# Thirteen more one-element activations at the head of ScalarE's stream, with written-out engine orders found anew

## The chip, the cores and the metric

The kernel runs on one core of one Trainium2 chip. A core has TensorE (PE; its weight loads are listed as PEld), VectorE (DVE), ScalarE (ACT), GpSimd (POOL) and SyncE (SP), which run their own instruction streams side by side and wait for one another through semaphores; SyncE and ScalarE also issue transfers (DMA) between the chip's main memory and the on-chip memories. The metric is the time of one execution on the device in microseconds (us).

## What is computed

Two 5-tap convolutions over time, each followed by a GELU and by taking every second row, then a joint of a speech transducer. With B = 2, T = 4000, D = 512, K = 5 and U = 8, all in bf16:

```python
h = sum(xp[:, i:i+T] @ w1[i] for i in range(5));  h = gelu(h)[:, ::2]     # T1 = 2000 rows
f = sum(hp[:, i:i+T1] @ w2[i] for i in range(5)); f = gelu(f)[:, ::2]     # T2 = 1000 rows
fe = f @ w_f;  ge = g @ w_g
j = tanh(fe[:, :, None, :] + ge[:, None, :, :])                           # B x 1000 x 8 x 512
out = j @ w_o
```

## The kernel before

**The start.** SyncE loads the first 512 rows of x (`xr`) and the first weights. TensorE runs eight dummy matmuls on constants, then transposes `xr` (`turn`, lines 567 to 587) into PSUM, the accumulator memory. VectorE and ScalarE copy the transposes to `eo`: VectorE the first part, ScalarE three copies. The first two of those, with VectorE's, are what the first real matmuls read (`direct`, line 766, tap 0); the third is read later, with taps 1 and 3. ScalarE runs one activation of a single element ahead of that (`warm`, line 499: it writes `warm[0:1]` from `warm[1:2]`, a scratch), which also loads the table of the GELU.

**The convolutions.** Most of both convolutions is computed by a fast algorithm on sums and differences of rows and of tap weights. `w1part` (line 631) and `w2part` (line 611) make the weights: `tt` steps on VectorE, and doublings (`scaled`, line 606) that either ScalarE or VectorE may run. `Triple.step` (line 669) makes the sums of rows (tiles `row`, `xp`, `xa`), again with doublings of either engine. A `Unit` (line 699) is one block of 128 output channels: five groups of matmuls into two PSUM banks, evicted between them by ScalarE (tile `sd`, then the GELU into `hT`) and VectorE (`acc`, `sd`).

**The joint.** ScalarE makes the tanh tiles `jT` and `jX`. The product with `w_o` is done on blocks of 4 x 128 rows by a seven-product scheme (`Seven`, line 1069): sums of tanh blocks (`sums`, tile `ss`) on GpSimd or VectorE, sums of `w_o` (`tw`), seven products on TensorE, results kept in `sn` or written to the output tile `og` by ScalarE or VectorE, and stores of `og` issued by SyncE. Single blocks of 128 rows in between go straight (`Plain`, tile `ost`). At the end (lines 1268 to 1273) the last `Seven` splits its last store between ScalarE's queue and SyncE's, and the last 128 columns of the last plain block are evicted and stored by ScalarE.

**What sets the order.** The program first records every step with what it reads and writes (`Plan`), and works out from that which step waits for which: a step waits for the semaphore of any step, of its own engine too, whose result it reads or whose tile it overwrites (`edges`, line 155). The order in which each engine runs its steps is not that of the recording: it is written out in full in `ORDER` (line 16), one list for each engine, as differences of step numbers. A step that may run on either of two engines (`flex`) runs on the one in whose list it stands. So an engine's list says both what it runs and in which order, and a step that has to wait holds up all behind it on its engine.

Of the kernel before, what the change touches and what calls it, by code (L numbers as in the profile page):

```python
# [7 lines left out]
ACT = mybir.ActivationFunctionType  # L8
# [6 lines left out]

ORDER = {
    "pe": """
# [13 lines left out]
        1 6 3 3 1 4 2 3""",  # L31
    "act": """
# [8 lines left out]
        91 -68 101 -95 96 -83 -8 25 -3 32 -23 25 -36 16 8 3 14 6 5 9 3 10 6 21 -8 14 10 3 10 6 10 3 8 6 6 3 12 7 1 8 1""",  # L41
    "dve": """
# [9 lines left out]
        -13 19 18 74 -52 -13 20 16 -9 6 -27 43 7 6 2 19 -7 13 15 -3 9 8 2""",  # L52
    "pool": """
        1 42 1 -42 1 1 1 15 218 1 -217 258 -252 253 8 89 174 150 1 54 -2 1 -31 33 33 2 -1 38 -36 35 40 -38 37 34 2 33
        -32 33 32 -30 31 1 1 33 1 28 1 1 28 155 -154 1 27 2 -1 33 -31 32 1 28 2 -1 31 -29 30 1 26 37 -36 37 1 1 33 34
        -33 34 -32 33 1 29 2 -1 33 2 -1 33 -31 32 1 34 2 35 2 27 -26 27 1 1 24 1 28 -26 29""",
    "sp": """
        6 2 1 1 1 1 1 1 1 1 1 1 1 2 2 1 1 1 1 2 1 1 1 1 1 248 1 1 1 1 1 1 2 1 1 1 1 1 254 1 1 145 3 33 33 4 1 1 30 4 33
        4 1 1 33 4 31 4 1 1 29 4 29 4 1 1 29 4 25 4 1 1 25 4 25 4 1 1 27 4 27 4 1 1 25 4 25 4 1 1 19 1 11 4 21 11 4 19
        11 4 17 11 1 1 4 17 11 1 1 4 17 11 4 1 1 19 11 4 21 1 11 4 25 4 23 1 1 4 23 4 19 1 1 7 3 3 5 5""",  # L60
}
# [254 lines left out]
def bass_standalone__seq2seq_rnn_t_joint__speech_kernel(  # L316
# [35 lines left out]
    BU = B * U  # L352
    NT = 512
    NWARM = 8
    TAPS = (0, 4, 2, 1, 3)
    NX = 2

    with ExitStack() as es:
        cur = [16512]

        def at(name, shape, dtype, offset=None):
            o = cur[0] if offset is None else offset
            b = Buf(nc, name, shape, dtype, o)
            if offset is None:
                cur[0] = (b.end + 31) // 32 * 32
            return b
# [29 lines left out]
        warm = at("warm", [2], FP32)  # L396
# [52 lines left out]
        def act(o, i, func, scale=1.0, bias=None):  # L449
            rd = (i,) if bias is None else (i, bias)  # L450
            pl.op("act", lambda e: e.activation(o.ap, i.ap, func, scale=scale,  # L451
                                                bias=0.0 if bias is None else bias.ap), rd, (o,),
                  o.ap.free_size() * 0.833e-3 + (0.05 if i.psum else 0.105 if bias is None else 0.186))
# [22 lines left out]
        def load_w(eng, dst, src, slack=0.0):  # L476
            return pl.dma(eng, lambda e: e.dma_start(dst.ap, src), (), (dst,), slack=slack)
# [4 lines left out]
        def load_xr(rt, after=None):  # L482
            n = NR[rt]
            dst = xr[rt][0:n].map(lambda a: a.rearrange("p r k c -> p (r k c)"))
            src = x[0, 4 * P * rt:4 * P * rt + n * P, :].rearrange("(p r) c -> p (r c)", r=n)
            o = pl.dma("sp", lambda e: e.dma_start(dst.ap, src), (), (dst,), nbytes=n * P * 1024, rate=370e3)  # L486
            if after is not None:
                o.after.append(after.idx)
            return o
# [6 lines left out]
            return pl.dma("sp", lambda e: e.dma_start_transpose(out=dst.ap, in_=src), (), (dst,), nbytes=n * 2 * D, rate=175e3, slack=slack)  # L496

        came = [load_xr(0)]
        act(warm[0:1], warm[1:2], ACT.Gelu_apprx_tanh)

        def load_w1(i, after=None):
            o = load_w("sp", w1_sb[i], w1[i].rearrange("(k c) d -> c k d", c=P), 0.5 if i == TAPS[1] else 0.2)
            if after is not None:
                o.after.append(after.idx)
            return o
# [3 lines left out]
        def load_a(*phs, after=None):  # L509
            for ph in phs:  # L510
                o = load_x6(xa, 0, ph, JA, 0, 16 * -(-(NF + 2) // 16), 0.8)
                if after is not None:
                    o.after.append(after.idx)

        came.append(load_w1(TAPS[0]))
        came.append(load_w1(TAPS[1]))
        came.append(load_xr(1, came[0]))
        came.append(load_w1(TAPS[2], came[0]))
        load_a(4, 0, after=came[1])
        came.append(load_w1(TAPS[3], came[-3]))  # L520
        load_a(2)
        came.append(load_w1(TAPS[4], came[-3]))
        load_a(1, 3, 5)
# [22 lines left out]
        def warm_mm(n):  # L546
            one = nc.const_aps.tensor(1.0, [P, NT], BF16)
            zz = View(one, np.zeros(0, np.int64), False)
            z = zz.map(lambda a: a[:, 0:P])
            for i in range(n):  # L550
                mm(ps.cols(0, NT), [(z, zz)], True, True)
                pl.ops[-1].cost = 0.43

        warm_mm(NWARM)
        psb = ps.h[:, :].bitcast(BF16)
# [748 lines left out]
```

## Time and profile before

| what | us |
|---|---|
| median of 3 runs (251.9 to 252.15) | 252.02 |
| the profiled execution | 251.77 |
| its span, first to last instruction | 249.9 |
| TensorE busy | 243.4 |
| VectorE busy | 207.8 |
| ScalarE busy | 196.8 |
| GpSimd busy | 100.6 |

The profile is of one execution. Its times count from the start of the span; the rest of the execution's own time, 1.9 us, lies outside the span. Busy time leaves out instructions that only wait or that issue transfers; the rows of issues have a q behind the engine (SPq, ACTq). A timeline row has the start, the length, the engine, the line of the kernel, the operation, and tiles written and read; in brackets stands the time that the engine idled before it and what it waited for. A row with x3 merges three instructions. The granted clock of TensorE was full throughout (0.999).

### The profile page before, as it was taken

How to read it: one execution, taken by the hardware profiler on the slowest of the kernel's cores; microseconds unless marked ns; L12 is line 12 of the kernel's file. 1: busy time of each engine (PE TensorE's matmuls, PEld its weight loads, DVE VectorE, ACT ScalarE, POOL GpSimd, SP SyncE). 2: the span in 40 equal slices, each digit the busy share in tenths (PEclk: the TensorE clock that was granted, in tenths of full speed). 3: DMA queues.
4: the chain of work that ended last, by engine and by line, in shares of the span. 5: the costliest groups of instructions: out<-in, count | busy, mean ns of one | idle time of the engine just before them, and what ended most of it. 6: DMA issues, size and time to landing. Idle time of an engine off the chain costs nothing.

```text
span 249.9 us, 5265 instructions
## 1 busy us (share of the span) xinstructions
PE 243.4 (97%) x1938; PEld 182.9 (73%) x1944; DVE 207.8 (83%) x369; ACT 196.8 (79%) x338; POOL 100.6 (40%) x107
## 2 busy tenths in 40 slices
PE   7999999999999999999999999999999999999992
PEld 3979976666666666666557887777888877878872
DVE  1799996967999993996857989769999999996962
ACT  4787868458795575533799999999999999997661
POOL 1000000000000000000008998969899999998510
PEclk9999999999999999999999999999999999999999
DMA  7999999999000070000001142232453656455465
GB/s 243 295 216 180 175 182 172 188 161 357 8 3 0 0 244 12 0 3 0 1 3 42 64 150 84 88 111 99 147 171 122 198 160 211 132 192 163 146 204 165
DMA packets 54871, 31.83 MB, mean 127 GB/s; under 512 B 31902, under 2 KB 54590, under 8 KB 54846
## 3 DMA queue, kind: packets, MB, share of 16 engines
q1 hardware_dynamic: 54558, 31.34, 47.7%
q8 instruction: 15, 0.25, 0.5%
q10 hardware_dynamic: 288, 0.16, 0.2%
q14 instruction: 10, 0.08, 0.1%
HBM read 7.60 MB, written 16.38 MB: 96 GB/s over the span
## 4 chain that ended last, share of the span: by engine, by line
PE 88%; ACT 5%; DMA 2%; DVE 1%; issue 1%; ACTq 1%; SPq 0%; DVEq 0%
PE acc L459 88%; ACT jT L451 2%; DMA w_sb<-in_w_dram 2%; ACT og L560 1%; ACT sn L560 1%; ACT jX L451 1%; ACTq L1037 1%; DVE og L446 1%; DVE sn L561 0%; DVE og L561 0%; PE acc L596 0%; SPq L486 0%; ACT ost L451 0%; DVEq L277 0%; ACTq L277 0%
## 5 line engine op out<-in xcount | busy, mean ns | idle before, releaser
L446 DVE TENSOR_TENSOR og<-acc,sn 128x512 bf16<-128x512 f32 x84 | 54.9, 680 | 6.6 <-PE acc L459 6.4
L451 ACT ACTIVATE jT<-feT,geT 128x1000 bf16<-128x1000 f32 (+5 forms) x60 | 57.4, 1015 | 0.3 <-DVE feT L446 0.3
L1091 POOL TENSOR_TENSOR ss<-jT 128x512 f16<-128x512 bf16 x34 | 39.4, 1176 | 35.2 <-DVE ss L1091 33.4
L459 PE MATMUL acc<-tw,ss 128*128 128x256 f16 x336 | 46.4, 273 | 0.0
L459 PE MATMUL acc<-row,w_sb 128*128 128x334 bf16 (+2 forms) x224 | 39.0, 297 | 0.0
L459 PEld LDWEIGHTS acc<-tw,ss 128*128 128x128 f16 x336 | 32.4, 98 | 7.5 <-ACT sn L560 0.5
L459 PE MATMUL acc<-wo_sb,jT 128*128 128x256 bf16 (+1 forms) x205 | 33.3, 283 | 0.2
L560 ACT ACTIVATE sn<-acc 128x512 f32<-128x512 f32 x49 | 30.3, 626 | 3.0 <-PE acc L459 2.8
L451 ACT ACTIVATE hT<-acc 128x334 bf16<-128x334 f32 (+3 forms) x36 | 15.4, 432 | 16.6 <-PE acc L459 16.0
L459 PEld LDWEIGHTS acc<-row,w_sb 128*128 128x128 bf16 x224 | 21.3, 97 | 9.2 <-DVE acc L602 0.7
L561 DVE COPY sn<-acc 128x512 f32<-128x512 f32 x35 | 23.8, 683 | 4.5 <-PE acc L459 4.2
L451 ACT ACTIVATE sd<-acc 128x334 f32<-128x334 f32 (+2 forms) x48 | 20.6, 432 | 6.3 <-PE acc L459 4.9
L459 PEld LDWEIGHTS acc<-wo_sb,jT 128*128 128x128 bf16 x208 | 20.3, 98 | 5.0
L443 POOL MEMSET hT<- 128x8 bf16 (+2 forms) x6 | 0.8, 148 | 55.2 <-ACT hT L451 42.9
L1091 POOL TENSOR_TENSOR ss<-ss,jT 128x512 f16<-128x512 f16 x18 | 21.0, 1172 | 2.7 <-DVE ss L1091 2.3
L1091 POOL TENSOR_TENSOR ss<-jT,ss 128x512 f16<-128x512 bf16 x17 | 20.0, 1177 | 2.1 <-DVE ss L1091 2.1
L446 DVE TENSOR_TENSOR row<-row 128x1336 bf16<-128x1336 bf16 (+2 forms) x24 | 18.9, 803 | 0.0
L602 DVE SCALAR_TENSOR_TENSOR acc<-acc,sd 128x334 f32<-128x334 f32 (+2 forms) x24 | 11.7, 486 | 8.1 <-PE acc L459 8.0
L451 ACT ACTIVATE jX<-feT,geT 128x1000 bf16<-128x1000 f32 (+3 forms) x20 | 18.2, 956 | 0.0
L459 PE MATMUL acc<-xp,w_t 128*128 128x334 bf16 (+1 forms) x96 | 17.6, 305 | 0.0
L459 PE MATMUL acc<-hT,w_t 128*128 128x334 bf16 x96 | 17.6, 304 | 0.0
L459 PE MATMUL acc<-wo_sb,ss 128*128 128x256 bf16 x112 | 17.3, 273 | 0.0
(130 smaller groups left out, 469.7 us busy)
## 6 DMA issues: line engine op xcount, KB each, us to landing
out_dram<-og SPq DMA_DIRECT2D x42, 256.0 KB, 2.2
w_sb<-in_w_dram SPq DMA_DIRECT2D x10, 512.0 KB, 5.9
out_dram<-og SPq DMA_DIRECT2D x14, 128.0 KB, 2.0
out_dram<-ost SPq DMA_DIRECT2D x10, 128.0 KB, 2.0
xr<-in_x_dram SPq DMA_DIRECT2D x1, 512.0 KB, 3.6
wf_sb<-in_w_f_dram SPq DMA_DIRECT2D x1, 512.0 KB, 4.1
wg_sb<-in_w_g_dram SPq DMA_DIRECT2D x1, 512.0 KB, 5.2
wo_sb<-in_w_o_dram SPq DMA_DIRECT2D x1, 512.0 KB, 7.6
```

The lines of the kernel that those rows point to most:

```text
L443: pl.op("pool", lambda e: e.memset(v.ap, 0.0), (), (v,))
L446: pl.op(eng, lambda e: e.tensor_tensor(out=o.ap, in0=a.ap, in1=b.ap, op=op), (a, b), (o,), 0.02 + 2.14e-3 * o.ap.free_size() if eng == "po ...
L451: pl.op("act", lambda e: e.activation(o.ap, i.ap, func, scale=scale, bias=0.0 if bias is None else bias.ap), rd, (o,), o.ap.free_size() * ...
L459: ins = e.matmul(o.ap, lhsT=l.ap, rhs=r.ap, start=start and n == 0, stop=stop and n == len(pairs) - 1, skip_group_check=not check)
L560: pl.flex({"act": (lambda e: e.activation(o.ap, v.ap, ACT.Copy), 0.05 + n * 0.833e-3), "dve": (lambda e: e.tensor_copy(out=o.ap, in_=v.ap) ...
L561: "dve": (lambda e: e.tensor_copy(out=o.ap, in_=v.ap), 0.065 + n * 1.04e-3)}, (v,), (o,))
L602: pl.op(eng, lambda e: e.scalar_tensor_tensor(out=o.ap, in0=a.ap, scalar=f, in1=b.ap, op0=ALU.mult, op1=add), (a, b), (o,), vec_cost(o, (a ...
L1037: pl.dma(eng, lambda e, s=s, dst=dst: e.dma_start(dst, s.ap), (s,), (), sem_of(key), 2 * n * P * 4)
L1091: fn = lambda e, o=S[i], x=x, y=y, op=op: e.tensor_tensor(out=o.ap, in0=x.ap, in1=y.ap, op=op)
```

## The change

`NPRE = 14` one-element activations stand where one stood. All later steps of the recording have numbers 13 higher, and the five written-out orders are new.

```diff
@@ bass_standalone__seq2seq_rnn_t_joint__speech_kernel
     NWARM = 8
+    NPRE = 14
     TAPS = (0, 4, 2, 1, 3)
...
         came = [load_xr(0)]
-        act(warm[0:1], warm[1:2], ACT.Gelu_apprx_tanh)
+        for _ in range(NPRE):
+            act(warm[0:1], warm[1:2], ACT.Gelu_apprx_tanh)
@@ ORDER, the head of ScalarE's list and the tail of GpSimd's
     "act": """
-        7 41 2 7 37 6 3 3 -41 50 9 9 -16 2 -5 12 2 -5 12 -3 9 -51 1 1 1 65 11 15 -23 16 -40 25 41 -39 31 -15 9 -23 26 6
...
+        7 1 1 1 1 1 1 1 1 1 1 1 1 1 41 2 7 37 6 3 3 -41 50 9 9 -16 2 -5 12 2 4 9 -6 -45 1 1 1 65 11 15 -23 16 -15 41 -8
...
-        -33 34 -32 33 1 29 2 -1 33 2 -1 33 -31 32 1 34 2 35 2 27 -26 27 1 1 24 1 28 -26 29""",
+        -33 34 -32 33 1 29 2 -1 33 2 -1 33 2 -1 35 2 -1 36 2 -1 28 -26 27 1 27 1 27 1 1""",
```

With the shift of 13 taken out, the lists of before and after compare so (steps by their numbers of before):

| engine | steps before, after | what differs |
|---|---|---|
| TensorE | 696, 696 | the order of eight steps in the first 37 us and of a dozen in the last 32 us |
| ScalarE | 339, 350 | 13 new activations; the order of a dozen steps from 15 to 37 us and of some twenty-five from 206 us on; hands over doublings 123 and 240 and evictions 1412, 1448, 1470, 1573; takes evictions 1397, 1400, 1434, 1533 |
| VectorE | 369, 371 | the order of some forty steps from 11 to 36 us and of some thirty from 215 us on; takes the six steps that ScalarE hands over and hands over the four that it takes; takes sums 1394, 1530, 1554, 1555, 1583 from GpSimd |
| GpSimd | 103, 103 | the order of the last seventeen; takes sums 1462, 1499, 1556, 1584, 1585 from VectorE |
| SyncE | 138, 138 | nothing |

Step 123 is the doubling of a block of tap 1 (`w1part`, line 649); step 240 is the doubling of one row block for the third `Triple` (`step`, line 673). Among VectorE's moved steps, the sums of taps 1 and 3 (`w1part`, lines 647 and 648) change places with row sums (`step`, line 687): three of them now come directly behind the row step that began at 15.76 us. Late in the program, VectorE's output additions of step numbers 1540, 1553 and 1569 (tile `og`) stand behind steps that they preceded.

More of the change, by code (lines that the diff above doesn't have):

```diff
@@ L28 @@
         1 2 1 2 1 2 1 2 7 1 2 1 3 1 7 1 2 1 2 1 2 1 2 7 1 2 1 3 1 5 1 2 1 2 1 2 1 2 7 1 2 1 5 1 5 1 2 1 2 1 2 1 2 7 1 2
[2 rows of a table removed]
-        1 6 3 3 1 4 2 3""",
[2 rows of a table added]
+        4 2 3""",
     "act": """
[8 rows of a table removed]
-        91 -68 101 -95 96 -83 -8 25 -3 32 -23 25 -36 16 8 3 14 6 5 9 3 10 6 21 -8 14 10 3 10 6 10 3 8 6 6 3 12 7 1 8 1""",
-    "dve": """
[9 rows of a table removed]
-        -13 19 18 74 -52 -13 20 16 -9 6 -27 43 7 6 2 19 -7 13 15 -3 9 8 2""",
[9 rows of a table added]
+        3 12 7 1 8 1""",
+    "dve": """
[9 rows of a table added]
+        7 6 17 67 -61 18 -37 46 35 -29 4 17 36 -10 3 -36 13 16 27 7 -21 27 15 -3 9 8 2""",
     "pool": """
-        1 42 1 -42 1 1 1 15 218 1 -217 258 -252 253 8 89 174 150 1 54 -2 1 -31 33 33 2 -1 38 -36 35 40 -38 37 34 2 33
+        1 55 1 -55 1 1 1 28 218 1 -217 258 -252 253 8 89 174 150 1 54 -2 1 -31 33 33 2 -1 38 -36 35 40 -38 37 34 2 33
         -32 33 32 -30 31 1 1 33 1 28 1 1 28 155 -154 1 27 2 -1 33 -31 32 1 28 2 -1 31 -29 30 1 26 37 -36 37 1 1 33 34
-        -33 34 -32 33 1 29 2 -1 33 2 -1 33 -31 32 1 34 2 35 2 27 -26 27 1 1 24 1 28 -26 29""",
+        -33 34 -32 33 1 29 2 -1 33 2 -1 33 2 -1 35 2 -1 36 2 -1 28 -26 27 1 27 1 27 1 1""",
     "sp": """
-        6 2 1 1 1 1 1 1 1 1 1 1 1 2 2 1 1 1 1 2 1 1 1 1 1 248 1 1 1 1 1 1 2 1 1 1 1 1 254 1 1 145 3 33 33 4 1 1 30 4 33
+        6 15 1 1 1 1 1 1 1 1 1 1 1 2 2 1 1 1 1 2 1 1 1 1 1 248 1 1 1 1 1 1 2 1 1 1 1 1 254 1 1 145 3 33 33 4 1 1 30 4 33
         4 1 1 33 4 31 4 1 1 29 4 29 4 1 1 29 4 25 4 1 1 25 4 25 4 1 1 27 4 27 4 1 1 25 4 25 4 1 1 19 1 11 4 21 11 4 19
```

47 rows, old and new, of the table ORDER are left out of this document.

## Prediction

> **What bounds the kernel now.** I read the page first, for the engines' shares and the chain that ended last.
>
> ```profile
> span 249.9 us, 5265 instructions
> PE 243.4 (97%) x1938; PEld 182.9 (73%) x1944; DVE 207.8 (83%) x369; ACT 196.8 (79%) x338; POOL 100.6 (40%) x107
> PE 88%; ACT 5%; DMA 2%; DVE 1%; issue 1%; ACTq 1%; SPq 0%; DVEq 0%
> ```
>
> TensorE is busy for 97% of the span, and 88% of the chain is its matmuls. Their number and shapes do not change. So time can be won or lost in three places only: before the first real matmul, in holes between matmuls, and after the last one. Busy time by stretch (time, then PE, PEld, DVE, ACT, POOL with their counts) shows how much room the other engines leave.
>
> ```profile
> 20.00:30.00 10.00, 10.00 (x115) 10.00 (x113) 9.81 (x23) 8.64 (x20) 0.24 (x2) 1.00 1.14 181
> 240.00:250.00 10.00, 5.33 (x45) 4.03 (x43) 3.99 (x8) 2.90 (x6) 0.00 (x0) 0.98 0.53 171
> ```
>
> From 20 to 30 us TensorE and VectorE are both full. At the end nothing is full: TensorE works 5.33 us of the last ten. The chain of work, in order of time, says what the end waits for, and the timeline of the last microseconds gives the neighbours.
>
> ```profile
> 244.95 2.44 ACTq L1037
> ...
> 247.50 0.28 ACT ost L451
> ```
>
> ```profile
> 244.12 1.26 PE L459 MATMUL acc<-wo_sb,jX 128*128 128x256 bf16 x12
> 244.94 0.38 SPq L1037 DMA_DIRECT2D out_dram<-og  x1
> 245.65 0.33 SPq L1037 DMA_DIRECT2D out_dram<-ost  x1
> 247.80 0.34 ACTq L1037 DMA_DIRECT2D out_dram<-ost  x1
> ```
>
> TensorE ends at 245.38 (244.12 + 1.26). ScalarE's last eviction (ost, 128x128) could start then, but stands behind a store that ScalarE itself issues, and that issue lasts 2.44 us, against 0.38, 0.33 and 0.34 us for the three others here. It releases ScalarE at 247.39, so the last store is issued at 247.80 and the program ends 2.15 us later. About 2.06 us (2.44 less 0.38) of the end is this one long issue.
>
> **Why that issue is long, as far as the trace tells.** The DMA view of just this stretch (244.95 to 247.39 us):
>
> ```profile
> GB/s 369 353 336 370 286 353 403 336 265 353 290 319 315 256 248 407 336 302 386 302 261 143 42 0 29 197 319 420 369 302 336 185 51 17 34 17 34 0 0 0
> q14 instruction: 1, 0.01, 0.8%
> out_dram<-og SPq DMA_DIRECT2D x1, 128.0 KB, 2.4
> ```
>
> Then the instruction queues of the whole program; two issues of SyncE, each followed by the instruction queue that moves something beside it (143.45 to 143.75 and 177.0 to 177.5 us); and the busy times of one stretch around another transfer:
>
> ```profile
> q8 instruction: 15, 0.25, 0.5%
> q14 instruction: 10, 0.08, 0.1%
> 143.49 2.21 SPq L1037 DMA_DIRECT2D out_dram<-og  x1
> q8 instruction: 1, 0.02, 37.2%
> 176.45 1.28 SPq L1037 DMA_DIRECT2D out_dram<-og  x1
> q14 instruction: 1, 0.01, 6.2%
> 187.00:187.40 0.40, 0.40 (x6) 0.29 (x3) 0.40 (x2) 0.40 (x2) 0.18 (x1) 1.00 0.78 271
> ```
>
> Instructions arrive by DMA: 15 transfers on one queue and 10 of 8 KB on the other. Exactly one of the ten falls inside the long issue. SyncE's two longest issues of stores, 2.21 and 1.28 us, also lie beside instruction transfers. The other eight transfers of q14 fall beside compute: in the 0.40 us around each, as around 187.0 us here, ScalarE and VectorE are busy for 0.38 to 0.40 us. They stall nothing. My reading is that a DMA issue is held while the block that follows it is being fetched, and an ordinary instruction is covered by the one that is executing. In the built program ScalarE's stream grows from 462 to 477 instructions of 64 bytes, and the long issue moves from the 454th to the 469th place. An 8 KB block is 128 instructions, so the boundary now comes some 15 instructions ahead of that issue, around 236 us, among evictions.
>
> [...]
>
> **The change part by part.** *The fourteen activations.* Thirteen are new. All write the same element, so each waits for the one before. Rows: the tiny activation of before, the next ScalarE work, a pair on VectorE of which the second waits for the first, and TensorE's weight load for the first real matmul.
>
> ```profile
> 2.03 0.20 ACT L451 ACTIVATE warm<-warm 128x1 f32<-128x1 f32 x1
> 4.89 0.66 ACT L451 ACTIVATE eo<-acc 128x256 bf16<-128x256 bf16 x2 [2.66 <-PE acc L575]
> 7.29 1.67 ACT L608 ACTIVATE hw<-w_sb 128x512 bf16<-128x512 bf16 x3 [0.81 <-DMA w_sb<-in_w_dram]
> 39.44 0.52 DVE L602 SCALAR_TENSOR_TENSOR acc<-acc,sd 128x336 f32<-128x336 f32 x1 [2.48 <-PE acc L459]
> 39.99 0.51 DVE L446 TENSOR_TENSOR sd<-acc,sd 128x336 f32<-128x336 f32 x1
> 6.02 0.35 PEld L459 LDWEIGHTS acc<-eo,w_sb 128*128 128x128 bf16 x4 [0.78 <-ACT eo L451]
> ```
>
> The wait between dependent steps is 0.03 us (39.99 less 39.96). So a tiny step takes 0.23 to 0.24 us, and thirteen take 3.0 to 3.1. The cover is the 2.66 us that ScalarE waits for TensorE's transposes. The last tiny step ends at 2.23 + 3.1 = 5.3, and the first copy starts at 5.2 to 5.35 in place of 4.89. The first two copies, which end at 5.55 (4.89 + 0.66), gate the first real matmul; they now end at 5.9 to 6.0. TensorE's weight load comes at 6.02, and needs a weight that lands shortly before. So the step costs 0 to 0.05 us; I take 0. The third copy is made good in the 0.81 us that ScalarE waits ahead of 7.29. If the dependent step were free, nothing changes; if it costs 0.28 us, the first matmul is 0.5 us late, and everything behind it.
>
> *The first 40 us in the new order.* On SyncE nothing changes place; GpSimd changes only late. Eight steps of TensorE, some forty of VectorE and a dozen of ScalarE do. Two doublings go from ScalarE to VectorE: a w_t (line 649) around 15 us and a row (line 673) around 36 us. The second falls into VectorE's idle 2.48 us ahead of 39.44 and costs nothing. The first lands in a full stretch. On VectorE, the step that needs the last tap's weights (w_t, line 648) moves up to stand right behind the row step of 15.76, and seven steps come ahead of the first unit's evictions.
>
> ```profile
> 7.63 0.29 DVE L609 TENSOR_SCALAR hw<-w_sb 128x512 bf16<-128x512 bf16 x1
> 10.41 0.58 SPq L477 DMA_DIRECT2D w_sb<-in_w_dram  x1
> w_sb<-in_w_dram SPq DMA_DIRECT2D x1, 512.0 KB, 6.3
> 15.76 0.59 DVE L446 TENSOR_TENSOR row<-row,xa 128x832 bf16<-128x832 bf16 x1
> 16.77 0.42 DVE L446 TENSOR_TENSOR w_x<-w_sb 128x512 bf16<-128x512 bf16 x1
> 27.91 0.38 DVE L602 SCALAR_TENSOR_TENSOR acc<-acc,sd 128x206 f32<-128x206 f32 x1 [0.18 <-PE acc L459]
> 30.03 0.85 DVE L446 TENSOR_TENSOR xp<-xp 128x1344 bf16<-128x1344 bf16 x1
> 30.94 0.46 PE L459 MATMUL acc<-xp,w_x 128*128 128x336 bf16 x2
> ```
>
> The doubling adds up to 0.29 us on VectorE. The last tap's weights land at 10.41 + 6.3 = 16.71. Before, their first use was at 16.77. Now it is next at about 16.5 (15.76 + 0.59 and most of 0.29), so VectorE waits some 0.2 us. Of these 0.5 us the idle 0.18 us at 27.91 absorbs a part, and the rest, 0.2 to 0.3 us, reaches the xp step of 30.03. That step ends at 30.88, and the matmul that reads it starts at 30.94: no slack. The other gates, by the same sums (the sd additions, the w_x of the third unit, the row differences), come up to 0.1 us late but ahead of 30.94 and are part of the same delay. So TensorE loses 0.2 us (bounds 0 and 0.35), and, being full, does not make it good.
>
> *The last 35 us in the new order.* Four evictions go from VectorE to ScalarE and four the other way, five sums go from GpSimd to VectorE and five back.
>
> ```profile
> 200.00:220.00 20.00, 19.89 (x160) 15.73 (x162) 19.54 (x33) 20.00 (x27) 20.00 (x18) 1.00 0.52 169
> L560 ACT ACTIVATE sn<-acc 128x512 f32<-128x512 f32 x24 | 14.9, 621 | 3.0 <-PE acc L459 2.8
> L561 DVE COPY sn<-acc 128x512 f32<-128x512 f32 x11 | 7.5, 681 | 0.7 <-PE acc L459 0.6
> ```
>
> An eviction costs 0.62 us on ScalarE and 0.68 on VectorE, so the exchange is even. TensorE has only 0.11 us of holes from 200 to 220 us, which bounds what better orders can win. Laid out by these durations, each eviction still ends before the matmul that needs its bank, the tightest by under 0.1 us. I take 0.1 us of loss (bounds: 0.1 gained, 0.6 lost).
>
> *The end.* With the issue at 0.38 us, ScalarE is free at 245.33, evicts at 245.42, and issues its last store at 245.75. Then SyncE's 128 KB store of 245.65 is last. The last store of before, 32 KB, took 2.15 us from issue to the end; 96 KB more, at the 330 GB/s of the stretch, take 0.3 us, and ScalarE's two stores, which now share that time, up to 0.5. The end is 245.65 + 2.15 + 0.3 = 248.1 to 248.6; I take 248.4, so 1.5 us are won (bounds 0 and 1.8).
>
> *Sum.* 0 + 0.2 + 0.1 - 1.5 = -1.2 us. The profiled execution took 251.77 us, 1.87 more than its span, so its like would take 250.6. The median of the runs is 252.02, 0.25 above it, by which I would say 250.8. I predict 250.7 us.
>
> **The rivals.** *The long issue stays.* It is the first store that ScalarE issues, and may be slow for that reason; no other first issue on that queue is in the trace. For it: the boundary of a block need not stall anything, since the eight transfers beside compute stalled nothing. Against it: SyncE's first issue takes no more than its others, and its two longest lie beside instruction transfers. Then only the 0.3 us are left: 252.02 + 0.3 = 252.3.
>
> *Tiny steps beyond the cover, and the long issue stays* (the slower side). The place is the first copy, and the point from which it decides is 0.24 us for a dependent tiny step: each 0.01 above it delays the first matmul by 0.13. At 0.28 us it is 0.5 us, and the time 252.02 + 0.3 + 0.5 = 252.8. For it: the cover is used up to within 0.1 us. Against it: the 0.03 us between dependent steps.
>
> *The gain is half eaten at the end.* In the new order VectorE makes three output additions of the groups before the last 3 to 5 us later, and SyncE issues its stores in a fixed order, so some 1.5 MB leave between 238 and 243 us, which at 330 GB/s is 4.5 us of full queues; or an eviction misses its matmul. At 0.8 us of cost the time is 251.5.
>
> **How the numbers follow.** The forecast, 250.7, gets 0.58; the issue that stays, 252.3, gets 0.24; both that and the late start, 252.8, get 0.08; the half-eaten gain, 251.5, gets 0.10. A measurement of this kernel can tell some 0.2% from no change, so faster is below 251.5 and slower above 252.5. The forecast and half of the last case are faster: 0.63. Three quarters of the issue that stays are within 0.2%, and with the other half of the last case that makes 0.23. The late start and the last quarter of the issue that stays are slower: 0.14. The range runs from the best bounds of the terms, 250.0 (1.8 won, 0 lost, from the profiled execution), to 252.4, where the second case is mostly in.
>
> **What would show it.** Right: an issue of ScalarE's store of about 0.4 us around 245.2, the last ScalarE eviction right behind TensorE's end, a chain that ends with a SyncE store, and one instruction transfer near 236 us among evictions. The start is right if the first real matmul is at 6.05 to 6.1 and the first 336-column matmul at 31.1 to 31.2. Wrong: an issue still of 2.4 us with no instruction transfer in it (a slow first issue), a first real matmul after 6.3, or holes on TensorE after 216 us of over 0.3 us.

## The result, and the profile after

The changed kernel takes **250.52 us** (median of 4 runs, 250.43 to 250.88) against 252.09 us for the kernel before in the same comparison (4 runs, 251.9 to 252.21). The ratio is 0.9944, with a 95% interval of 0.9932 to 0.9955. That is 1.57 us less in the medians. The profiled executions differ by 1.22 us (251.77 and 250.55), and it is these that can be taken apart. First the page of the changed kernel: the span, the busy times and the shares of the chain that ended last.

```profile
span 248.7 us, 5271 instructions
PE 243.8 (98%) x1938; PEld 182.6 (73%) x1944; DVE 208.0 (84%) x371; ACT 197.6 (79%) x349; POOL 100.7 (41%) x107
PE 86%; ACT 7%; DMA 2%; issue 1%; DVE 1%; SPq 0%; DVEq 0%; ACTq 0%
```

The share of ACTq (ScalarE's DMA issues) in the chain is 0%, where the kernel before had 1%. The last steps of the chain of work and the timeline of the last microseconds show why (start, duration, engine, line, what).

```profile
242.61 3.01 PE acc L461 x23
...
245.65 0.28 ACT ost L453
```

```profile
244.34 1.26 PE L461 MATMUL acc<-wo_sb,jX 128*128 128x256 bf16 x12
...
245.16 0.39 SPq L1040 DMA_DIRECT2D out_dram<-og  x1
245.17 0.38 ACTq L1040 DMA_DIRECT2D out_dram<-og  x1
245.65 0.28 ACT L453 ACTIVATE ost<-acc 128x128 bf16<-128x128 f32 x1 [0.51 <-PE acc L461]
245.87 0.33 SPq L1040 DMA_DIRECT2D out_dram<-ost  x1
245.96 0.35 ACTq L1040 DMA_DIRECT2D out_dram<-ost  x1
```

The issue that took 2.44 us takes 0.38. The last eviction now waits for TensorE (0.51 us, released by its last matmul) and not for ScalarE's own store. TensorE's last group starts at 244.34 in place of 244.12, so everything ahead of the end has become 0.22 us longer. From TensorE's end to the end of the span it is 3.13 us (245.60 to 248.73), where it was 4.57 (245.38 to 249.95): 1.44 us won. 1.44 - 0.22 is the 1.22 us of the profiled executions.

Where the instruction transfer went is seen in two short stretches of the DMA view: 238.2 to 238.8 us, and the issue itself, 245.17 to 245.55 us.

```profile
q14 instruction: 1, 0.01, 4.5%
```

```profile
q1 hardware_dynamic: 149, 0.14, 104.9%
```

In the issue there is only the stores' own queue. The 8 KB transfer that lay in it is at 238.41 us, among evictions, and nothing stalls there: from its start to its end at 238.85 us, TensorE, VectorE and ScalarE are each busy for the whole 0.44 us. The two traces also tell which of the ten 8 KB transfers are ScalarE's. Six begin within 0.5 us of where they began before. Four have moved with its stream, from 40.76, 122.73, 187.10 and 245.87 us to 30.35, 111.84, 182.17 and 238.41 us; in both traces the last of them begins when 448 of ScalarE's rows (waits and issues counted) have started. The long issue was the 448th row, and the short one is the 463rd. (The built program counts six instructions more ahead of each: 454 and 469.)

The start, on ScalarE, and TensorE's first real matmuls:

```profile
2.03 3.25 ACT L453 ACTIVATE warm<-warm 128x1 f32<-128x1 f32 x14
5.18 1.55 ACT L453 ACTIVATE eo<-acc 128x256 bf16<-128x256 bf16 x3
7.83 1.67 ACT L611 ACTIVATE hw<-w_sb 128x512 bf16<-128x512 bf16 x3 [1.10 <-DMA w_sb<-in_w_dram]
```

```profile
5.88 1.38 PE L461 MATMUL acc<-eo,w_sb 128*128 128x254 bf16 x11 [0.69 <-ACT eo L453]
```

Fourteen dependent steps fill 3.25 us. The first copy follows without a gap, 0.29 us later than before, and it now releases the first matmul, at 5.88 us. Before, the first weights released it, at 6.05:

```profile
6.05 1.15 PE L459 MATMUL acc<-eo,w_sb 128*128 128x254 bf16 x9 [0.64 <-DMA w_sb<-in_w_dram]
```

### The profile page after: what moved, and what is told of

The parts are those of the page before. It is cut to its first block, busy times and chain, and to the rows that moved or that the text cites. A ratio compares the mean times of both kernels' runs of the same rounds, so it can differ in the third digit from the quotient of the medians.

```text
span 248.7 us, 5271 instructions
## 1 busy us (share of the span) xinstructions
PE 243.8 (98%) x1938; PEld 182.6 (73%) x1944; DVE 208.0 (84%) x371; ACT 197.6 (79%) x349; POOL 100.7 (41%) x107
## 4 chain that ended last, share of the span: by engine, by line
PE 86%; ACT 7%; DMA 2%; issue 1%; DVE 1%; SPq 0%; DVEq 0%; ACTq 0%
PE acc L461 86%; ACT jT L453 3%; DMA w_sb<-in_w_dram 2%; ACT sn L563 1%; ACT og L563 1%; ACT jX L453 1%; DVE og L448 1%; ACT sd L453 1%; DVE sn L564 0%; DVE og L564 0%; PE acc L599 0%; ACT fT L453 0%; SPq L479 0%; SPq L488 0%; ACT ost L453 0%
## 5 line engine op out<-in xcount | busy, mean ns | idle before, releaser
L563 ACT ACTIVATE sn<-acc 128x512 f32<-128x512 f32 x48 | 29.7, 628 | 3.4 <-PE acc L461 2.8
L564 DVE COPY sn<-acc 128x512 f32<-128x512 f32 x36 | 24.6, 685 | 6.3 <-PE acc L461 6.0
L1094 POOL TENSOR_TENSOR ss<-ss,jT 128x512 f16<-128x512 f16 x19 | 22.3, 1179 | 2.4 <-DVE ss L1094 1.9
L1094 POOL TENSOR_TENSOR ss<-jT,ss 128x512 f16<-128x512 bf16 x15 | 17.5, 1169 | 2.4 <-DVE ss L1094 2.4
```

The costliest lines, as they stand in the source:

```text
L563: pl.flex({"act": (lambda e: e.activation(o.ap, v.ap, ACT.Copy), 0.05 + n * 0.833e-3), "dve": (lambda e: e.tensor_copy(out=o.ap, in_=v.ap) ...
L564: "dve": (lambda e: e.tensor_copy(out=o.ap, in_=v.ap), 0.065 + n * 1.04e-3)}, (v,), (o,))
L1094: fn = lambda e, o=S[i], x=x, y=y, op=op: e.tensor_tensor(out=o.ap, in0=x.ap, in1=y.ap, op=op)
```

## Theories and experiments

**Theory P (place).** The issue was long because it stood at the place of ScalarE's stream where the next 8 KB block of instructions is fetched. The tiny activations are worth something only as a shift. **Rival O (order):** the new order changed what runs and leaves beside the issue. **Rival F (first):** the first store of ScalarE's queue is slow by itself; the changed kernel's own trace, with a first store of 0.38 us, already speaks against it. For the 0.22 us lost ahead of the end, **E** (the early orders) stands against **L** (the landing of the first loads, which differs by execution); **T, C, D** and **S** are refinements that came up on the way.

### 1. The shift alone

```diff
-    act(warm[0:1], warm[1:2], ACT.Gelu_apprx_tanh)
+    for _ in range(14):
+        act(warm[0:1], warm[1:2], ACT.Gelu_apprx_tanh)
     # ORDER as before, indices behind 7 shifted by 13
```

> The kernel before with its own order of steps on every engine, and only the thirteen additional tiny activations behind the first one. ScalarE's first store moves from the 454th to the 467th place of its stream. Theory P (place: the issue is long because it stands where ScalarE's next 8 KB block of instructions is fetched): the issue takes about 0.38 us, the program ends about 3.1 us behind TensorE's last matmul as in the changed kernel (before: 4.57 us), the time is 252.09 - 1.47 = 250.6 us, and down to 250.3 us if the new orders' 0.22 us come off the changed kernel's 250.52. Theory O (order: the issue became short because the new order changed what runs and leaves beside it): the issue stays at 2.4 us and the time is 252.1 to 252.2 us. Theory F (the first store of ScalarE's queue is slow by itself) also gives 2.4 us. For the start: the first real matmul comes within 0.1 us of the kernel before if the thirteen steps (0.234 us each) are covered.

Measured: 250.81 us (6 runs, 250.16 to 251.78) against 252.37 (12 runs), ratio 0.9932 (0.9905 to 0.9959). The end, in the timeline:

```profile
246.16 0.38 ACTq L1044 DMA_DIRECT2D out_dram<-og  x1
246.64 0.28 ACT L457 ACTIVATE ost<-acc 128x128 bf16<-128x128 f32 x1 [0.51 <-PE acc L465]
```

The old orders with the shift have the short issue, and the span ends 3.13 us behind TensorE (246.59 to 249.72), as in the changed kernel. Theories O and F fall. The first real matmul starts at 5.88 us, 0.17 ahead of the kernel before, so the thirteen steps cost nothing there. This execution is late by another cause: TensorE is 1.2 us behind the kernel before by the first matmul of 336 columns. One piece of that is a wait for weights:

```profile
17.56 0.33 PE L465 MATMUL acc<-eo,w_sb 128*128 128x378 bf16 x1 [0.17 <-DMA w_sb<-in_w_dram]
```

Another wait for a load follows on VectorE:

```profile
28.34 0.87 DVE L452 TENSOR_TENSOR row<-row,xp 128x1352 bf16<-128x1352 bf16 x1 [0.63 <-DMA xp<-in_x_dram]
```

The orders are those of before, so these waits are no effect of an order. They are the first sign of theory L.

### 2. The orders alone

```diff
-    NPRE = 14
+    NPRE = 1
     # ORDER of the changed kernel, indices behind 7 shifted back by 13
```

> The changed kernel with one tiny activation in place of fourteen; its orders of steps are kept. ScalarE's first store stands at the 456th place, two behind that of the kernel before. Theory O: the issue takes 0.38 us and the time is that of the changed kernel, 250.5 us. Theory P: the place where the block is fetched now lies on the eviction two instructions ahead, about 0.6 us earlier. If the fetch holds whatever issue stands behind it until it is complete (2.44 us from reaching the place), the issue takes about 1.8 us and the time is 252.1 + 0.2 - 0.6 = 251.7 us; if only the instruction at the place itself is held, the issue takes 0.38 us and the time is 250.5 us.

Measured: 251.2 us (7 runs, 250.72 to 251.52), ratio 0.9946 (0.9923 to 0.9969).

```profile
245.12 1.72 ACTq L1043 DMA_DIRECT2D out_dram<-og  x1
246.95 0.28 ACT L456 ACTIVATE ost<-acc 128x128 bf16<-128x128 f32 x1 [1.85 <-DMA out_dram<-ost]
```

The issue is still long, 1.72 us, close to the 1.8 us of theory P with a hold that goes on until the fetch is complete. (The bracket of the eviction names a store; ScalarE itself was held by its issue until 246.85.) The two places that this order happens to shift the stream are worth the 0.72 us by which the issue is shorter. The time, 251.2 us, lies between the two forecasts, 250.5 and 251.7, and the medians differ by 1.17 us from the kernel before; where the rest of that comes from is not shown.

### 3. One place

```diff
-    act(warm[0:1], warm[1:2], ACT.Gelu_apprx_tanh)
+    for _ in range(2):
+        act(warm[0:1], warm[1:2], ACT.Gelu_apprx_tanh)
```

> The kernel before with one additional tiny activation: everything on ScalarE one place later, orders unchanged. Theory P: the fetch falls on the short wait just ahead of the issue. If the fetch holds what stands behind it, the issue still takes 1.8 to 2.4 us and the time is 251.9 to 252.1 us; if only the very place is held, 0.38 us and 250.6 us. Theory O and theory F: 2.4 us, 252.1 us.

Measured: 251.08 us in one run.

```profile
245.16 1.56 ACTq L1043 DMA_DIRECT2D out_dram<-og  x1
```

One place changes the issue by 0.88 us, with the orders untouched. It was expected between 1.8 and 2.4 us if held and is 1.56: the transfer came at 245.03, ahead of the issue. The time is below the 251.9 to 252.1 us of that case too; it is one run.

### 4. A whole block

```diff
-    act(warm[0:1], warm[1:2], ACT.Gelu_apprx_tanh)
+    for _ in range(129):
+        act(warm[0:1], warm[1:2], ACT.Gelu_apprx_tanh)
```

> The kernel before with 128 additional tiny activations, orders unchanged: ScalarE's first store stands 128 places later, one whole 8 KB block. Theory P: it is again at the place of a fetch and takes about 2.4 us. A theory by which any shift of the stream, or more instructions ahead of it, make the issue short, gives 0.38 us. For the start: the first copy begins at 2.03 + 129 x 0.234 = 32.2 us in place of 4.89, so the whole is some 27.3 us longer, 279.4 us with the long issue and 277.9 us without it, less what the late start saves in waits for loads (up to 1 us).

Measured: 279.89 us in one run (279.4 expected).

```profile
2.03 30.21 ACT L459 ACTIVATE warm<-warm 128x1 f32<-128x1 f32 x129
32.15 1.55 ACT L459 ACTIVATE eo<-acc 128x256 bf16<-128x256 bf16 x3
...
273.11 2.42 ACTq L1046 DMA_DIRECT2D out_dram<-og  x1
```

At 128 places the long issue is back, 2.42 us, with a transfer of 8 KB at 274.01 in it. A shift as such does not cure it: the place counts, and 128 instructions on it comes again. The trace has eleven transfers of 8 KB in place of ten, one more for 128 instructions more (64 bytes each, by this quotient), and the last begins when 576 of ScalarE's rows have started, 128 more than in the kernel before. The time itself is no close comparison: TensorE's mean granted clock was 0.951 in this run, against 0.999 in the kernel before. The same rows price the tiny step: 129 of them in 30.21 us, 0.234 us each from start to start.

### 5 to 8. The parts of the orders, on one chip

Four kernels share the runs of the kernel before (252.22 us, 26 runs).

```diff
 5: the changed kernel again
 6: NPRE = 14  ->  NPRE = 8, ORDER of the changed kernel
 7: NPRE = 8, early part of ORDER from before, last part from the changed kernel
 8: NPRE = 8, ORDER of before throughout
```

> The changed kernel once more, as the yardstick of the three beside it on the same chip. Two views of its first 30 us compete. Theory E (early orders): in the changed kernel TensorE ran 0.08 us behind the kernel before at its 144th matmul and 0.30 us behind at its 300th, and this is the price of the new early orders. Theory L (landings): it is the landing of the first loads, which differs from one execution to the next; with the orders of before but more tiny activations TensorE was 0.15 to 1.2 us behind too (0.21 with one more, 1.21 with thirteen more). For this run both expect 250.5 us and an issue of 0.38 us; theory E a delay between the 144th and the 300th matmul of 0.2 us again, theory L one that differs.

> The changed kernel with eight tiny activations in place of fourteen. ScalarE's first store stands at the 463rd place, nine behind that of the kernel before, and the place of the fetch lies on an eviction about 3 us ahead of it. By the theory of the place, the hold (2.44 us from reaching the place) is over by then and the issue takes 0.38 us; a theory by which it takes all fourteen gives up to 2.4 us. The tiny activations end 1.4 us earlier (six times 0.234), so the first copy waits for TensorE again. If fourteen are covered the time is that of the changed kernel beside it, within 0.05 us; if the first copy was late, it is up to 0.1 us less.

> As the run with eight tiny activations, but every engine has the order of the kernel before up to the middle of the program and the new order in the last 35 us. Issue 0.38 us by the theory of the place. Theory E: 0.2 to 0.3 us less than the run with eight tiny activations and both new orders. Theory L: no difference that exceeds the spread of the runs.

> The kernel before with seven additional tiny activations and its own orders throughout. ScalarE's first store stands at the 461st place, seven behind. Issue 0.38 us by the theory of the place. The late orders alone tell it from the run with the late orders: there TensorE won 0.08 us in the last 35 us of the changed kernel's profile, so this one is expected 0.1 us slower than that, with the bounds of the prediction 0.6 us faster and 0.1 us slower. Theory O gives 252.1 us.

| run | us (median, range, runs) | ratio to before (95%) | issue us | hole at 22.9 to 23.2 us | delay, 144th to 288th matmul (counted from 0) |
|---|---|---|---|---|---|
| 5: changed, 14 tiny | 250.70 (250.01 to 252.05, 9) | 0.9929 (0.9897 to 0.9961) | 0.38 | 0.18 | 0.30 |
| 6: changed, 8 tiny | 250.82 (250.06 to 253.36, 12) | 0.9936 (0.9909 to 0.9963) | 0.40 | 0.22 | 0.34 |
| 7: early orders of before, 8 tiny | 250.40 (250.05 to 253.02, 12) | 0.9941 (0.9909 to 0.9973) | 0.38 | none | 0.28 |
| 8: all orders of before, 8 tiny | 250.46 (250.05 to 250.81, 6) | 0.9920 (0.9889 to 0.9950) | 0.38 | none | 0.08 |

The issue is short in all four, at four distances from the place (15, 9, 10 and 7 instructions). The times do not tell the orders apart: the lowest runs are 250.01 to 250.06 in all four, and the ranges overlap. The traces do, in part. The hole (time from one matmul's start to the next above its usual 0.09 us) is in every execution with the new early orders, and in none with the old. The delay over a longer stretch does not separate them: 0.28 us in run 7 and 0.63 in run 1 with old early orders, 0.08 in run 8. So both theories hold a part: E some 0.1 to 0.25 us, L from 0 to more than the whole effect. The traces show L as VectorE's wait for rows of x: 0.63 us in run 1 (at 28.34) and 0.21 us in run 7 (at 27.93), and none in runs 3, 5, 6 and 8.

The start with eight tiny activations (run 6):

```profile
2.03 1.84 ACT L456 ACTIVATE warm<-warm 128x1 f32<-128x1 f32 x8
5.02 1.70 ACT L456 ACTIVATE eo<-acc 128x256 bf16<-128x256 bf16 x3 [1.15 <-PE acc L581]
```

```profile
5.79 1.91 PE L464 MATMUL acc<-eo,w_sb 128*128 128x254 bf16 x16
8.01 0.72 PE L464 MATMUL acc<-eo,w_sb 128*128 128x254 bf16 x5 [0.32 <-DMA w_sb<-in_w_dram]
```

With eight, ScalarE waits 1.15 us for TensorE again, and the first matmul comes 0.09 us earlier than with fourteen (5.88); in run 7, with eight as well, it comes at 5.89, released by the weights. Run 6 gains nothing by it: TensorE then stands for the second weights, 0.32 us, at 8.01.

### 9. Four places: is it time or count?

```diff
-    act(warm[0:1], warm[1:2], ACT.Gelu_apprx_tanh)
+    for _ in range(5):
+        act(warm[0:1], warm[1:2], ACT.Gelu_apprx_tanh)
```

> The kernel before with four additional tiny activations, orders unchanged: ScalarE's first store stands at the 458th place, four behind. In the runs so far the long issue ended 1.19 to 1.21 us behind the end of the 8 KB transfer, whatever its own start (places 454, 455, 456 and 582). Theory T (time): the hold is over 1.2 us after the transfer; the place of the fetch now lies on the eviction that starts at 243.2 to 243.4 us, so the transfer comes at 243.4 to 244.3 us, the hold ends at 245.0 to 246.0 us, and the issue, which starts at about 245.1, takes 0.38 to 0.9 us. Theory C (count: an issue within a few places behind the fetch waits the full time): 1.6 to 2.4 us. Time 250.3 to 251.2 us by theory T.

Measured: 251.58 us in one run, with TensorE late by landings as in run 1 (VectorE waits 0.60 us for rows of x at 28.2 us). The DMA view of 243.6 to 244.5 us, and the issue:

```profile
q14 instruction: 1, 0.01, 4.9%
```

```profile
246.06 0.38 ACTq L1043 DMA_DIRECT2D out_dram<-og  x1
```

The transfer lasts from 243.69 to 244.40. A hold of 1.2 us behind it is over at 245.6, and the issue starts at 246.06 and takes 0.38. Theory C (1.6 us or more at so few places) falls, and theory T stands. The time missed its expectation, 250.3 to 251.2 us, by the landings, not by the end.

### 10. Another store at the place

```diff
-    for t, eng in ((2 * r, "act"), (2 * r + 1, "sp")):
+    for t, eng in ((2 * r, "sp"), (2 * r + 1, "sp")):
```

> The kernel before, unshifted, with one store given from ScalarE's queue to SyncE's: the one that was issued for 2.44 us. On ScalarE the last eviction now stands at the place of the fetch and the last store (32 KB) one place behind it, and this store is the first that ScalarE issues. Theory T: the hold passes on to that store; the fetch is reached between 244.4 and 245.0 us, the hold ends between 246.2 and 247.4 us, and the issue, which starts at about 245.75, takes 0.5 to 1.7 us. A theory by which the 128 KB store itself was slow gives 0.34 us; theory F (the first store on ScalarE's queue) 2.4 us. SyncE's additional issue (0.38 us) moves its last store to about 246.0 us. Time 250.4 to 251.2 us by theory T.

Measured: 250.85 us in one run. The timeline, and the DMA view of the issue (245.63 to 247.30 us):

```profile
245.63 1.66 ACTq L1043 DMA_DIRECT2D out_dram<-ost  x1
```

```profile
q14 instruction: 1, 0.01, 1.2%
```

The last store, of 32 KB, took 0.34 us in the kernel before and takes 1.66 now that it stands one place behind the fetch. The hold does not belong to the 128 KB store. In this run it passes to the store that stands there.

### 11 and 12. One doubling

```diff
 11: ORDER of the changed kernel, 8 tiny activations; step 123 (w_t): "dve" -> "act"
 12: ORDER of before, 8 tiny activations; step 123 (w_t): "act" -> "dve"
```

> The run with eight tiny activations and both new orders, with one step of the early order put back: the doubling of weights (a w_t, at about 15 us) is done by ScalarE as before and not by VectorE. In all four profiles with the new early orders TensorE has a hole of 0.10 to 0.25 us at 22.9 to 23.2 us, ahead of the matmuls that read a row step of VectorE (which ends at 22.7 to 22.8 us, VectorE having been busy without a gap since 16 us); in none of the five with the early orders of before. Theory D (the doubling, 0.3 us of VectorE's time): no hole there, below 0.03 us. Theory S (the sequence of VectorE's other steps): the hole stays, 0.05 us or more.

> The run with seven additional tiny activations and all orders of before, with that doubling alone given to VectorE, at the place that the new order gives it. Theory D: TensorE gets a hole of 0.1 to 0.25 us between 20 and 24 us. Theory S: none there; the 0.3 us then show, if at all, at the steps that had no slack, around 30 us (0 to 0.3 us).

Run 11 takes 250.19 us, run 12 251.87 us (one run each; the kernel before beside them 252.18). In run 11 the group that stood in the hole follows the one ahead of it at the usual distance, and the matmuls of 336 columns start 0.06 us ahead of the kernel before:

```profile
22.28 0.52 PE L464 MATMUL acc<-xa,w_x 128*128 128x206 bf16 x4
22.63 0.52 PE L464 MATMUL acc<-row,w_t 128*128 128x206 bf16 x4
...
30.88 0.75 PE L464 MATMUL acc<-xp,w_x 128*128 128x336 bf16 x4
```

Without the doubling on VectorE the hole is gone, as theory D has it; theory S (0.05 us or more) falls for this hole. The delay from the 144th to the 288th matmul is 0.04 us, against 0.34 in run 6, which differs in this step alone. Run 12 is less clean. There is no hole from 20 to 24 us, where D expected one; holes of 0.13 us at 25.1 and 0.29 us at 30.0 are there instead, and ahead of the second VectorE itself waited for a load:

```profile
27.72 0.87 DVE L451 TENSOR_TENSOR row<-row,xp 128x1352 bf16<-128x1352 bf16 x1 [0.34 <-DMA xp<-in_x_dram]
```

So the doubling costs TensorE something in either order. Where it shows depends on the steps behind it, and how much of run 12's 0.56 us is the late load stays open.

## Why the prediction was right, point by point

Between the profiled executions the sum was forecast as -1.2 us and came out as -1.22. That it is so close is luck: the early orders cost 0.09 us more than forecast and the tail 0.18 less, and the delay at the first matmul of 336 columns differs by as much from one execution of the same kernel to the next (0.29 us here, 0.47 in run 5).

**The end** (-1.5 us, measured -1.44). That the place counts is shown: the shift alone makes the issue short (0.38 us, run 1), the orders alone don't (1.72, run 2), 128 places bring it back (2.42, run 4), and another store takes it over (1.66, run 10). What the prediction did not have is when the hold ends. In the five executions with a long issue, that is 1.19 to 1.21 us behind the end of the 8 KB transfer, whatever the issue's own start and size:

| execution | transfer ends | issue starts | issue ends | behind the transfer |
|---|---|---|---|---|
| before | 246.18 | 244.95 | 247.39 | 1.21 |
| 4: 128 places | 274.34 | 273.11 | 275.52 | 1.19 |
| 3: one place | 245.52 | 245.16 | 246.71 | 1.19 |
| 2: orders alone | 245.64 | 245.12 | 246.85 | 1.20 |
| 10: other store | 246.09 | 245.63 | 247.30 | 1.20 |

"Held while the block is being fetched" was therefore too short: the transfer itself lasts 0.31 us in the kernel before, 0.33 in run 4 and 0.49 in run 3, and 1.2 us follow. What holds the issue for those 1.2 us no trace shows. One supporting argument failed. SyncE's issues of 2.21 and 1.28 us were read as the same thing, but they lie beside transfers of 16 KB on the other instruction queue (143.48 to 145.26 and 176.00 to 177.36 us) and end 0.43 and 0.37 us behind those, not 1.2. The second has an 8 KB transfer in it as well (177.09 to 177.59), and ends 0.14 us behind that.

"A chain that ends with a SyncE store" was wrong by a hair: ScalarE's last 32 KB store, issued at 245.96, landed at 248.05, and SyncE's 128 KB store of 245.87 at 247.89. The transfer came at 238.4, not near 236: the fifteen places take some 7 us, not 9.

**The tiny activations** (0, bounds 0 and 0.05 us). A step takes 0.234 us, in the 0.23 to 0.24 that the prediction took from VectorE's dependent pair; the first copy starts at 5.18, just ahead of its 5.2 to 5.35. The first matmul came at 5.88 rather than 6.05, since the weights, whose landing released it before, were there by then. In run 6, with eight, it is 0.09 us earlier, which would put fourteen a little over the upper bound; but with eight it comes anywhere from 5.73 (run 8) to 5.89 us (run 7), so no cost of the count is shown, and in run 6 the wait for the second weights takes the 0.09 back.

**The early orders** (+0.2, between the profiles +0.29 at the first matmul of 336 columns). The cause named, a doubling that VectorE takes over, is borne out by run 11. One step of the working failed: that "VectorE waits some 0.2 us" for the last tap's weights. In the changed kernel it does not wait. The first two rows are VectorE around the last tap's weights (back to back, 16.82), the third is the row step that came late, the fourth the xp step; then TensorE's two gated groups.

```profile
16.23 0.59 DVE L448 TENSOR_TENSOR row<-row,xa 128x832 bf16<-128x832 bf16 x1
16.82 0.42 DVE L448 TENSOR_TENSOR w_t<-w_sb 128x512 bf16<-128x512 bf16 x1
...
22.18 0.58 DVE L448 TENSOR_TENSOR row<-row 128x824 bf16<-128x824 bf16 x1
...
30.31 0.86 DVE L448 TENSOR_TENSOR xp<-xp 128x1344 bf16<-128x1344 bf16 x1
```

```profile
22.91 0.52 PE L461 MATMUL acc<-row,w_t 128*128 128x206 bf16 x4
...
31.23 0.60 PE L461 MATMUL acc<-xp,w_x 128*128 128x336 bf16 x3
```

The row step of 22.18 ends at 22.76 and its matmuls start at 22.91, 0.10 us late: a gate eight microseconds ahead of the one that the prediction watched. The xp step of 30.31 ends at 31.17, and the matmul follows at 31.23, just above the 31.1 to 31.2 forecast. Of the 0.29 us, 0.08 lie ahead of the 48th matmul, where the second weights landed later (TensorE's loads of them wait 0.33 us ahead of 7.86, before not at all); 0.10 are the hole, and the rest comes in pieces of 0.02 to 0.04.

**The tail** (+0.1, measured -0.08). Here the sign was wrong, within its bounds. TensorE's delay against the kernel before falls from 0.30 us at 212 us to 0.22 at the end, and in run 2, with the same orders, from 0.26 to 0.18; in runs 1 and 3, with the old, it does not fall. The prediction's own row had 0.11 us of holes from 200 to 220 us as the most that could be won.

**The rivals.** The issue that stays is refuted. The late start with a dependent step of 0.28 us is refuted by 0.234. Of a gain half eaten by bunched stores nothing is seen: the span ends 3.13 us behind TensorE both with the old orders and with the new.

**A better version** is suggested, not shown: fewer tiny activations suffice (4, 7 and 13 more all gave an issue of 0.38 us, in runs 9, 8 and 1), and the doubling is better left on ScalarE. Run 11 has both, and its 250.19 us is one run; the changed kernel's own runs go from 250.01 to 252.05.

## What to carry to other kernels

A change that adds work can gain by its place alone (run 1: 250.81 us against 252.37): ask of each DMA issue near the end how many instructions stand ahead of it on its engine, and whether an instruction transfer lies inside its duration. Here four places more were enough: in run 9 the issue started 2.37 us behind the transfer's start and took 0.38 us. One place and two were not, with 1.56 and 1.72 us (runs 3 and 2). But the next edit that adds or removes an instruction moves the place again, and 128 more brought 2.42 us back (run 4), so such a gain is luck until it is looked after. And compare two orders by what recurs in several traces: here two executions of the same early order differed by more than the orders did.

## What the runs showed of the hardware that was not expected

- ScalarE's hold ended 1.19 to 1.21 us behind the transfer's end in five executions; in the same time SyncE's own issues went at 0.33 to 0.50 us (0.33 at 245.65 in the kernel before, 0.50 at 245.15 in run 3). What was held in these five was a DMA issue of ScalarE, with whose stream the transfer moves. Evictions of ScalarE were not: in the changed kernel two of them start at 238.72 and 239.53 us and take 0.59 and 0.60, during the transfer (238.41 to 238.85) and within 1.2 us of its end.
- A SyncE issue beside a transfer of ScalarE's was longer too, but not by a hold of 1.2 us behind it: in run 9 one took 0.88 us, where it takes 0.40 in the kernel before, and ended 0.15 us behind the transfer of 243.69 to 244.40:

```profile
243.67 0.88 SPq L1043 DMA_DIRECT2D out_dram<-og  x1
```

- SyncE's long issues end behind 16 KB transfers (2.21 and 1.28 us, 0.43 and 0.37 behind). In the changed kernel too, one of 1.77 us at 143.79 ends 0.42 us behind a 16 KB instruction transfer (143.72 to 145.13), while other SyncE issues of 0.33 to 0.39 us lie at the start of such transfers (219.64 and 205.36 us). There the next issue is the long one: 0.89 us at 220.44 and 0.96 us at 206.23, which end 0.39 and 0.41 us behind the transfer. Why this is so was not tried.
- The first loads vary: with the early orders of before, the first matmul of 336 columns started 0.08 us ahead of the profile before (run 10) to 1.2 us behind it (run 1).
